# Gated linear attention and a SiLU block on one core: TensorE in stated order for the late chunks, k turned by VectorE and DRAM, masks by ScalarE and GpSimd

## The chip, the cores and the metric

The kernel runs on one core of one Trainium2 chip. The metric is the device time of one execution in microseconds. Before the change it is 563.04 us, the median of three runs (562.8 to 563.6).

## What is computed

Two blocks in a row. The first is a recurrence over 768 tokens for each of 4 batches and 8 heads of dimension 48, with a state of 48x48 that decays by `alpha`:

```python
def _attn_ref(q, k, v, alpha):                      # each (4, 8, 768, 48)
    state = np.zeros((B, H, D, D), dtype=np.float32)
    for t in range(S):
        state = alpha[:, :, t, :, None] * state + np.einsum('bhd,bhe->bhde', k[:, :, t], v[:, :, t])
        y[:, :, t] = np.einsum('bhd,bhde->bhe', q[:, :, t], state)
    return y

def _moe_ref(x, w_in, w_out):                       # x (3072, 384), w_in (384, 2048), w_out (2048, 384)
    h = x @ w_in
    return (h * (1.0 / (1.0 + np.exp(-h)))) @ w_out
```

The output of the first, with batch and token as rows and head and dimension as columns, is the `x` of the second. The weights come as 64-bit floats and are converted on the chip.

## The kernel before

The kernel cuts the tokens into chunks of 128, which gives 24 chunks (6 in time for each of 4 batches), numbered so that chunk `n` is batch `n % 4` at time `n // 4`. A chunk's decays are cumulative products, made by a scan on VectorE. q is multiplied and k divided in such a way that the recurrence within a chunk becomes two matrix products: scores = k q (masked so that only earlier tokens count), and values = v times the masked scores, plus a product of the carried state with q. A third small product adds the chunk's k and v into the state. The second block follows in groups of four chunks. From the third group on, its first product is done with a scheme of 20 block products (`PRODUCTS`), and its second product with 7 (`leave`). All are in float32.

The program is written as a list of steps. In each step, four slots hold stages of attention, and behind each slot some pieces of the second block are filled in. Pools, semaphores and, where nothing keeps an instruction in program order, also the order of each engine's queue are set by the framework's scheduler. `NA` is 8: chunks 0 to 7 are loaded with tokens on the partitions and turned by TensorE; from chunk 8 on, q, k and alpha are loaded so that VectorE's 32x32 block transpose turns them.

The stages of attention that the change touches (cut):

```python
pe, dve, act, gps = nc.tensor, nc.vector, nc.scalar, nc.gpsimd
...
def turns(x, n):                                    # which of two buffers chunk n takes
    return x[(n + 1) % 2 if n < NA else 0]
...
def blank(n):                                       # chunks 8 on: clear two PSUM banks for the scores
    ps = ctxs[n]["blank"] = [ps_attn() for _ in range(2)]
    for t in ps:
        act.activation(t..., ident[:, 0:1].to_broadcast([128, 4 * C]), AF.Copy, scale=0.0)      # L741

def scores(n):
    ps = c.pop("blank") if n >= NA else [ps_attn() for _ in range(2)]
    for j in (0, 2, 1, 3):
        for e in range(2 if n >= NA else 1):
            for u in range(2):
                ...
                pe.matmul(ps[u][at, j, t], lhsT=c["kp"][r, j, at], rhs=c["qp"][r, j, t], ...)    # L757
    g = c["g"] = work.tile([128, 2, NP, C], F32, name="g")
    for u in range(2):
        if n < GB:                                  # chunks 0 to 3
            act.copy(g[:, u], ps[u])                                                             # L763
            gps.affine_select(g[:, u], g[:, u], ...)                                             # L764
            continue
        m = mask[:, :, None, :] if n >= NA else mask[:, 0:1, None, :]
        dve.tensor_tensor(g[:, u]..., ps[u]..., m.to_broadcast(...), ALU.mult)                   # L768
    if ci < NCH - 1:                                # all but the last chunk of each batch
        ps_k = ps_attn()
        for j in range(NP):
            pe.transpose(ps_k[:, j, :], c["kp"][:, j, :], ident)                                 # L774
        c["kn"] = work.tile([128, NP, C], F32, name="kn")
        act.copy(c["kn"], ps_k)                                                                  # L776
    ...
def values(n):                                      # 16 small matmuls, 28 with a state: L800
def states(n):                                      # 16 small matmuls into the state:   L815
```

From chunk 8 on, scores of later and earlier halves of a chunk are written only where the mask can keep something, so the banks are blanked before and multiplied by the mask afterwards.

The slots of a step, and the weights' conversion in the early steps:

```python
for slot, group in enumerate(stages):
    # steps from 8 on, with lag behind the step:
    # [[(scores, 1)], [(products, 0)], [(values, 1), (states, 1)], [(quotient, 0), (blank, 0)]]
    ...
    fill(step, slot)                                # pieces of the second block that are due

def weights(which):                                 # one piece of w_in or w_out for each next()
    up = ahead.pop() if ahead else rounding(bits)   # ScalarE, L609
    dve.tensor_scalar(...); dve.scalar_tensor_tensor(...); dve.tensor_tensor(w, w, up, ALU.add)
    if i + 1 < len(pieces):
        ahead.append(rounding(coming[0]))           # ScalarE, for the next piece
    ...
def store(...):                                     # in leave(): one of 48 outputs
    nc.sync.dma_start(out[r : r + C, c * HO : (c + 1) * HO], o)                                  # L996
```

Of the kernel before, what the change touches and what calls it, by code (L numbers as in the profile page):

```python
# [355 lines left out]
def quotients(  # L356
# [19 lines left out]
    nc = tc.nc  # L376
    pe, dve, act, gps = nc.tensor, nc.vector, nc.scalar, nc.gpsimd
    B, H, S, D = q.shape
# [27 lines left out]
    gpool = pool("gpool", 6)  # L406
    opool = pool("opool", 2)
    rpool = pool("rpool")
    upool = pool("upool")

# [106 lines left out]
    def turns(x, n):  # L517

        return x[(n + 1) % 2 if n < NA else 0]

# [8 lines left out]

    mask = consts.tile([128, 2, C], F32, name="mask")  # L530
    gps.memset(mask, 1.0)
    for odd in range(2):
        for e in range(2):
            m = mask[CH * e : CH * e + CH, odd, :]
            gps.affine_select(m, m, pattern=[[1, C]], compare_op=ALU.is_ge, fill=0.0,
                              base=-CH * (e ^ odd), channel_multiplier=-1)

# [56 lines left out]
    def weights(which):  # L594
# [18 lines left out]
        for i, (dst, src) in enumerate(pieces):  # L613
            if not wide:
                act.dma_start(dst, src)
                yield
                continue
            assert which == 0 or conv_done[0] == n_conv[0]
            bits = coming.pop(0)
            up = ahead.pop() if ahead else rounding(bits)  # L620
            hi, w = bits[:, :, 1], dst.bitcast(I32)
            tc.keep_in_program_order(
                dve.tensor_scalar(w, hi, 3, 0x3FFFFFFF, ALU.logical_shift_left, ALU.bitwise_and))
            dve.scalar_tensor_tensor(w, hi, -(1 << 30), w, ALU.bitwise_and, ALU.bitwise_or)
            dve.tensor_tensor(w, w, up, ALU.add)  # L625
            if i + 1 < len(pieces):
                ahead.append(rounding(coming[0]))
            fetch()
            yield
# [35 lines left out]

    xts, xcs, late = {}, {}, {}

# [8 lines left out]
    def products(n):  # L676
# [25 lines left out]
        dve.tensor_single_scalar(least[:, n, :], u[:, 0:end:W], 2.0**-64, ALU.max)  # L702
        kp = c["kp"] = turns(kps, n)
        ut = tokens(u)
# [13 lines left out]
    def quotient(n, sg=None, q=None):  # L718

        c = ctxs[n]  # L720
        if sg is None:
            if n < NA:
                return
            sg = c.pop("sg")
        end, iv = NP * W, inv
        dve.reciprocal(iv[:, 0:end:W], least[:, n, :])
        p = turns(qps, n)
        dve.tensor_tensor_scan(p[:, 0:end], sg[:, 0:end], iv[:, 0:end], 0.0, ALU.mult, ALU.add)  # L728
        qp = c["qp"] = tokens(p)
        if q is None:  # L730
            q = late["turn"].tile([128, NP, C], F32, name="turn")
            turned(c["q"], q)
        dve.tensor_tensor(qp, q, qp, ALU.mult)

    def blank(n):

        if n < NA:
            return
        ps = ctxs[n]["blank"] = [ps_attn() for _ in range(2)]
        for t in ps:  # L740
            act.activation(t.rearrange("p j c -> p (j c)"), ident[:, 0:1].to_broadcast([128, 4 * C]),  # L741
                           AF.Copy, scale=0.0)

    def scores(n):
        c = ctxs[n]
        ci, b = c["ci"], c["b"]
        ps = c.pop("blank") if n >= NA else [ps_attn() for _ in range(2)]

# [3 lines that stand above are left out]
# [4 lines left out]
                              start=True, stop=True)  # L758
        g = c["g"] = work.tile([128, 2, NP, C], F32, name="g")
        for u in range(2):  # L760
            if n < GB:

                act.copy(g[:, u], ps[u])  # L763
                gps.affine_select(g[:, u], g[:, u], pattern=[[0, NP], [1, C]], compare_op=ALU.is_ge,  # L764
                                  fill=0.0, base=0, channel_multiplier=-1)
                continue
            m = mask[:, :, None, :] if n >= NA else mask[:, 0:1, None, :]
            dve.tensor_tensor(g[:, u].rearrange("p (o j) c -> p o j c", o=2),  # L768
                              ps[u].rearrange("p (o j) c -> p o j c", o=2),
                              m.to_broadcast([128, 2, NP // 2, C]), ALU.mult)  # L770
        if ci < NCH - 1:
            ps_k = ps_attn()
# [12 lines left out]
    def values(n):  # L785

        c = ctxs[n]
        ci, b, g, qp = c["ci"], c["b"], c["g"], c["qp"]
        vn = c["v"].rearrange("p (j u) d -> p j (u d)", u=2)
        s = st[b].rearrange("p j u e -> p j (u e)")  # L790
        py = ps_attn()
        todo = [(3 * j + i, vn[:, j, at : at + 32], g[:, u, j, :])
                for j in range(NP) for i, at, u in ((0, 0, 0), (1, 32, 0), (2, 80, 1))]
        todo += [(3 * j + 1, vn[:, j, 48:80], g[:, 1, j, :]) for j in range(NP)]
        if ci > 0:
# [10 lines left out]
    def states(n):  # L806
        c = ctxs.pop(n)
        ci, b, vn = c["ci"], c["b"], c["v"]
        if ci < NCH - 1:

            ps = ps_attn()
            for j in range(NP):
                for i in range(4):
                    r = slice(32 * i, 32 * i + 32)
                    pe.matmul(ps[r, j, 0:D], lhsT=c["kn"][:, j, r], rhs=vn[:, 2 * j + i // 2, 0:D],  # L815
                              start=True, stop=True)
# [14 lines left out]
    def sums_x(grp):  # L831
        xcs[grp] = late["xc"].tile([128, len(SUMS_X), TB], F32, name="xc")
        for to, sa, a, sb, b in SUMS_X:
            combine(block_x(grp, to), sa, block_x(grp, a), sb, block_x(grp, b))
        yield
# [137 lines left out]
    def leave(grp, h):  # L973
# [14 lines left out]
        def store(m, c, x, y=None):  # L988
# [6 lines left out]
            r = b * S + ci * C  # L995
            nc.sync.dma_start(out[r : r + C, c * HO : (c + 1) * HO], o)  # L996

# [104 lines left out]

    marks = [2 * SLOTS + 2] + [(GB * i + 2 * GB) * SLOTS + 2 for i in range(len(phases))]

    def settle():
# [3 lines left out]
                    wx=pool("wx").tile([128, 8, NQ, 128], F32, name="wx"))  # L1109
        quads = pool("quads")  # L1110
        late["quads"] = {name: quads.tile([128, 32 + 4 * NP * D], F32, name=f"{name}t") for name in "akq"}
        for name, t in late["quads"].items():
# [3 lines left out]
    def fill(step, slot):  # L1116

        at = step * SLOTS + slot
        if at < marks[0]:
            if step >= 1:  # L1120
                convert(0, (at - SLOTS) * 3 // (marks[0] - SLOTS) + 1)
            return
# [10 lines left out]
    for step in range(STEPS):  # L1133
# [6 lines left out]
        elif step >= NA:  # L1140
            stages = [[(scores, 1)], [(products, 0)], [(values, 1), (states, 1)], [(quotient, 0), (blank, 0)]]
        for slot, group in enumerate(stages):
            for stage, lag in group:
# [6 lines left out]
                if stage is states and n + 1 + NIN < NA:  # L1150
                    load(n + 1 + NIN)
                if stage is quotient and n + 1 < NT:
                    load(n + 1)
                if stage is states and n + NV < NT:
                    load_v(n + NV)
            fill(step, slot)
            if step * SLOTS + slot >= NA * SLOTS - 1 and conv_done[1] == NFT and not late:
# [21 lines left out]
    ps = ps_attn()[0:1, 0, 0:1]  # L1179
    pe.matmul(ps, lhsT=good, rhs=mask[:, 0, C - 1 : C], start=True, stop=True)  # L1180
    dve.tensor_single_scalar(small, ps, 127.5, ALU.is_ge)
# [62 lines left out]
```

## Time and profile before

| | |
|---|---|
| Time, median of three | 563.04 us |
| Span of the profiled execution | 561.6 us |
| Instructions | 12,420 |
| DMA | 63.8 MB, 114 GB/s in the mean |
| Granted TensorE clock, mean | 0.994 |

The page of the profile has six parts: busy time by engine, the span in 40 slices, the DMA queues, the chain of work that ended last, the costliest groups of instructions, and the DMA issues. PE is TensorE's matmuls, PEld its weight loads, DVE VectorE, ACT ScalarE, POOL GpSimd, SP SyncE, whose queue issues the DMAs. "L774" is line 774 of the kernel before. The chain is 75% TensorE, 14% VectorE and 5% DMA. A float32 matmul of the large kind appears as two records, so a group "x16" of `ps_o` is one product of 8 matmuls, and a group "x12" of `ps_m` one of 6.

### The profile page before, as it was taken

What the parts mean: (1) busy time and instruction counts of PE and PEld (TensorE: products, weight loads), DVE (VectorE), ACT (ScalarE), POOL (GpSimd) and SP (SyncE); (2) the same over time, 40 slices, a digit from 0 to 9 for tenths busy, and PEclk for the clock granted to TensorE, in tenths of its full rate; (3) what the DMA queues carried; (4) which work ended last, traced back from release to release, by engine and by line L of the source; (5) the groups of instructions that cost most, each with busy time, mean ns of one, the idle gap of its engine ahead of it and who ended that gap; (6) DMA issues with size and microseconds to landing.
All of it is one profiled execution on the core that took longest, in us unless ns stands there. A gap on an engine that the chain in (4) does not pass through costs nothing.

```text
span 561.6 us, 12420 instructions
## 1 busy us (share of the span) xinstructions
PE 543.9 (97%) x5074; PEld 492.6 (88%) x5074; DVE 453.0 (81%) x829; ACT 205.3 (37%) x406; POOL 15.1 (3%) x36
## 2 busy tenths in 40 slices
PE   5899999999999999999999999999999999999996
PEld 3688887998999999899989999999998999899995
DVE  5797899966999799986998897899895875857731
ACT  2566543213233342443433443434443342332100
POOL 4211000100000000000000000000000000000000
PEclk9899999999999999999999999999999999999998
DMA  9989971143443333333425544435522123334200
GB/s 206 230 241 223 234 183 34 43 126 100 100 107 89 73 97 87 101 87 85 131 70 160 142 108 134 130 81 153 136 69 81 53 85 118 99 94 125 71 30 26
DMA packets 94417, 63.81 MB, mean 114 GB/s; under 512 B 55312, under 2 KB 86032, under 8 KB 94352
## 3 DMA queue, kind: packets, MB, share of 16 engines
q1 hardware_dynamic: 94352, 62.94, 43.3%
q8 instruction: 41, 0.67, 0.5%
q14 instruction: 24, 0.20, 0.1%
HBM read 58.20 MB, written 4.72 MB: 112 GB/s over the span
## 4 chain that ended last, share of the span: by engine, by line
PE 75%; DVE 14%; DMA 5%; SPq 2%; issue 2%; ACT 1%; POOL 0%; DVEq 0%; ACTq 0%
PE ps_o L980 33%; PE ps_m L882 18%; PE ps_m L858 11%; PE ps_a L800 6%; DMA bits<-in_moe_w_out_dram 3%; PE ps_a L757 3%; DVE seen L663 2%; PE ps_a L774 1%; DVE g L896 1%; DMA bits<-in_moe_w_in_dram 1%; DVE u L699 1%; PE ps_a L815 1%; DVE w_out L625 1%; DVE p L728 1%; SPq L456 1%
## 5 line engine op out<-in xcount | busy, mean ns | idle before, releaser
L980 PE MATMUL ps_o<-w_out,g 128*128 128x192 f32 x768 | 133.6, 328 | 1.1 <-DVE o L994 1.1
L980 PEld LDWEIGHTS ps_o<-w_out,g 128*128 128x128 f32 x768 | 125.5, 190 | 3.9 <-DVE o L994 1.5
L980 PE MATMUL ps_o<-wt,g 128*128 128x192 f32 x576 | 100.0, 327 | 0.0
L980 PEld LDWEIGHTS ps_o<-wt,g 128*128 128x128 f32 x576 | 95.1, 190 | 1.5
L858 PE MATMUL ps_m<-xt,w_in 128*128 128x256 f32 x384 | 88.5, 382 | 1.0 <-ACT xt L805 1.0
L858 PEld LDWEIGHTS ps_m<-xt,w_in 128*128 128x128 f32 x384 | 71.0, 190 | 11.0 <-ACT xt L805 1.4
L882 PE MATMUL ps_m<-xc,w_in 128*128 128x256 f32 x288 | 70.1, 379 | 0.0
L882 PEld LDWEIGHTS ps_m<-xc,w_in 128*128 128x128 f32 x288 | 54.0, 190 | 6.4 <-DVE g L896 0.2
L663 DVE TENSOR_REDUCE seen<-bits 128x1 f32<-128x384 int32 (+2 forms) x65 | 42.4, 689 | 16.8 <-DMA bits<-in_moe_w_out_dram 16.5
L893 ACT ACTIVATE g<-g 128x1024 f32<-128x1024 f32 x32 | 33.1, 1055 | 57.5 <-DVE g L896 57.5
L985 DVE TENSOR_TENSOR g<-g 128x512 f32<-128x512 f32 x72 | 48.5, 686 | 5.6 <-PE ps_o L980 5.6
L882 PE MATMUL ps_m<-xc,wx 128*128 128x256 f32 x192 | 50.1, 383 | 0.0
L888 ACT COPY g<-ps_m 128x512 f32<-128x512 f32 x64 | 36.8, 587 | 36.1 <-PE ps_m L882 36.0
L780 ACT ACTIVATE st<-st,least 128x96 f32<-128x96 f32 x80 | 24.1, 364 | 58.4 <-DVE least L702 58.4
L882 PEld LDWEIGHTS ps_m<-xc,wx 128*128 128x128 f32 x192 | 35.0, 190 | 4.2 <-issue 0.4
L896 DVE TENSOR_TENSOR g<-ps_m,g 128x512 f32<-128x512 f32 x56 | 37.4, 683 | 0.8 <-PE ps_m L882 0.5
L699 DVE TENSOR_TENSOR_SCAN u<-al,one 128x516 f32<-128x516 f32 x24 | 29.1, 1212 | 10.4 <-ACT al L696 10.3
L728 DVE TENSOR_TENSOR_SCAN p<-al,inv 128x516 f32<-128x516 f32 x24 | 29.4, 1226 | 5.2 <-PE ps_a L800 4.9
L861 ACT ACTIVATE g<-ps_m 128x512 f32<-128x512 f32 x32 | 19.0, 595 | 39.2 <-PE ps_m L858 39.0
L800 PE MATMUL ps_a<-g,vn 128*32 128x128 f32 x768 | 28.0, 282 | 3.9 <-POOL g L764 3.9
L800 PEld LDWEIGHTS ps_a<-g,vn 128*32 128x32 f32 x768 | 20.3, 112 | 11.2 <-issue 5.5
L768 DVE TENSOR_TENSOR g<-ps_a,mask 128x512 f32<-128x512 f32 x40 | 25.7, 685 | 4.0 <-PE ps_a L757 3.7
(125 smaller groups left out, 620.7 us busy)
## 6 DMA issues: line engine op xcount, KB each, us to landing
bits<-in_moe_w_in_dram SPq DMA_DIRECT2D x24, 512.0 KB, 4.7
bits<-in_moe_w_out_dram SPq DMA_DIRECT2D x32, 384.0 KB, 3.4
at<-in_alpha_dram SPq DMA_DIRECT2D x64, 96.0 KB, 2.4
kt<-in_k_dram SPq DMA_DIRECT2D x64, 96.0 KB, 2.6
qt<-in_q_dram SPq DMA_DIRECT2D x64, 96.0 KB, 2.5
bits<-in_alpha_dram SPq DMA_DIRECT2D x9, 512.0 KB, 3.8
out_dram<-o SPq DMA_DIRECT2D x48, 96.0 KB, 1.9
an<-in_alpha_dram SPq DMA_DIRECT2D x8, 192.0 KB, 5.1
```

What stands on the lines that cost most here:

```text
L663: dve.tensor_reduce(seen[kind][which][:, i : i + 1], x, axis=AX, op=op, apply_absolute_value=True))
L699: dve.tensor_tensor_scan(u[:, end - 1 :: -1], sg[:, end:0:-1], one[:, end:0:-1], 0.0, ALU.mult, ALU.add)
L728: dve.tensor_tensor_scan(p[:, 0:end], sg[:, 0:end], iv[:, 0:end], 0.0, ALU.mult, ALU.add)
L768: dve.tensor_tensor(g[:, u].rearrange("p (o j) c -> p o j c", o=2), ps[u].rearrange("p (o j) c -> p o j c", o=2), m.to_broadcast([128, 2, ...
L800: pe.matmul(py[32 * at : 32 * at + 32, t, :], lhsT=w, rhs=x, start=(i < 4), stop=(i >= len(todo) - 4), skip_group_check=True)
L858: pe.matmul(ps[:, e, :], lhsT=w_in[:, t, (f + e) * 128 : (f + e + 1) * 128], rhs=xt[:, t, :], start=(t == 0), stop=(t == NKT - 1))
L882: pe.matmul(ps[:, e], lhsT=block_w(w)[:, 2 * pair + e], rhs=block_x(grp, x), start=(first and e == 0), stop=(e == 1), skip_group_check=True)
L888: act.copy(to, ps)
L893: act.activation(x, x, AF.Silu)
L896: dve.tensor_tensor(to, a, b, op)
L980: pe.matmul(ps, lhsT=x, rhs=w[:, i], start=(first and i == 0), stop=(i == HF - 1), skip_group_check=True)
L985: dve.tensor_tensor(cells(grp, h, pair, *to), cells(grp, h, pair, *x), cells(grp, h, pair, *y), ALU.subtract)
```

## The change

The change has six parts:

1. From chunk 8's step on (as soon as `late` is filled), every TensorE instruction is kept in the order in which the program states it. Before that the scheduler still decides. The sums of `sums_x` on VectorE are kept in order too.
2. For chunks 8 to 19, k is no longer transposed by TensorE. VectorE transposes its 32x32 blocks (`flip`), one DMA writes them to DRAM, four DMAs read them back in the order that the states need (`land`), a step later.
3. The masks of chunks 4 to 7 are made like those of chunks 0 to 3. Those of chunks 8 to 23 are made by six ScalarE copies and four GpSimd selections; the part that nobody writes is set to zero once, so the blanking goes, and so does the mask tensor.
4. Outputs are issued by GpSimd's queue, except those of the last group.
5. The stages are arranged anew: quotient in the third slot; values, states and `flip` in the fourth. q gets a second buffer for the late chunks, and the marks by which pieces fall due move by one slot.
6. In the first steps, the first weight conversion of ScalarE is asked for on its own, before the rest.

It is for taking work off TensorE, and for giving it a queue whose order the author sets. The diff, cut to its core:

```diff
-    pe, dve, act, gps = nc.tensor, nc.vector, nc.scalar, nc.gpsimd
+    dve, act, gps = nc.vector, nc.scalar, nc.gpsimd
+    late = {}
+    def in_order(ins):
+        return tc.keep_in_program_order(ins) if late else ins
+    class pe:
+        @staticmethod
+        def matmul(*args, **kw):
+            in_order(nc.tensor.matmul(*args, **kw))
+        @staticmethod
+        def transpose(*args):
+            in_order(nc.tensor.transpose(*args))
...
-    opool = pool("opool", 2)
+    opool = pool("opool", 3)
+    dram = pool("dram", 2, bass.MemoryType.DRAM)
...
-    mask = consts.tile([128, 2, C], F32, name="mask")
-    gps.memset(mask, 1.0)
-    (four affine_selects on it)
+    decayed = fix.tile([128, 2 * NP * C], F32, name="g")
+    low, high = slice(0, CH), slice(CH, C)
+    earlier, later = [(low, 0), (high, 1)], [(low, 1), (high, 0)]
...
             up = ahead.pop() if ahead else rounding(bits)
+            if which == i == 0:
+                yield
...
-        p = turns(qps, n)
+        p = turns(qps if n < NA else [qps[0], late["p"]], n)
...
-    def blank(n): (two ScalarE activations into PSUM)
+    def flip(n):
+        if n < NA or c["ci"] == NCH - 1:
+            return
+        t = late["turn"].tile([128, NP, C], F32, name="turn").rearrange("p c (j d) -> p c j d", j=NP)
+        dve.transpose(t, c["kp"].rearrange("p j (c i) -> p c j i", i=32))
+        c["flip"] = dram.tile([128, NP * C], F32, name="flips")
+        nc.sync.dma_start(c["flip"], t.rearrange("p c j d -> p (c j d)"))
+    def land(n):
+        if "flip" in c:
+            c["kn"] = work.tile([128, NP, C], F32, name="kn")
+            x = c.pop("flip").rearrange("(r d) (i x) -> i d r x", r=4, i=4)
+            for i in range(4):
+                nc.sync.dma_start(c["kn"][32 * i : 32 * i + 32], x[i])
...
-        for u in range(2):
-            (chunks 0 to 3: ScalarE copy, GpSimd select; others: VectorE times mask)
-        if ci < NCH - 1:
+        for u in range(2 if n < NA else 0):
+            act.copy(g[:, u], ps[u])
+            gps.affine_select(g[:, u], g[:, u], pattern=[[0, NP], [1, C]], ...)
+        if n >= NA:
+            for u in range(2):
+                act.copy(swapped[:, :, u, :, CH:], ps[u][:, :, :, CH:])
+            for r, o in earlier:
+                for u in range(2):
+                    act.copy(swapped[r, o, u, :, 0:CH], ps[u][r, o, :, 0:CH])
+            for at, half in ((CH, later), (0, earlier)):
+                for r, o in half:
+                    x = swapped[r, o].rearrange("p u j c -> p (u j) c")[:, :, at : at + CH]
+                    gps.affine_select(x, x, pattern=[[0, NP], [1, CH]], ...)
+        if n < NA and ci < NCH - 1:
...
-            nc.sync.dma_start(out[r : r + C, c * HO : (c + 1) * HO], o)
+            (gps if grp < NG - 1 else nc.sync).dma_start(out[r : r + C, c * HO : (c + 1) * HO], o)
...
-    marks = [2 * SLOTS + 2] + [(GB * i + 2 * GB) * SLOTS + 2 for i in range(len(phases))]
+    marks = [2 * SLOTS + 2] + [(GB * i + 2 * GB) * SLOTS + 3 for i in range(len(phases))]
...
+            if at == SLOTS:
+                next(conv[0])
...
-            stages = [[(scores, 1)], [(products, 0)], [(values, 1), (states, 1)], [(quotient, 0), (blank, 0)]]
+            stages = [[(land, 1), (scores, 1)], [(products, 0)], [(quotient, 0)],
+                      [(values, 1), (states, 1), (flip, 0)]]
```

## The prediction

> **What bounds the kernel now.** I read the page from the top: shares of busy time, then the slices, then single stretches of the timeline. Part 1 of the page and three rows of its part 2 (each digit the busy tenths of one fortieth of the span, some 14 us):
>
> ```profile
> PE 543.9 (97%) x5074; PEld 492.6 (88%) x5074; DVE 453.0 (81%) x829; ACT 205.3 (37%) x406; POOL 15.1 (3%) x36
> ...
> PE   5899999999999999999999999999999999999996
> PEld 3688887998999999899989999999998999899995
> DVE  5797899966999799986998897899895875857731
> ```
>
> The reader is to see that TensorE (PE) has no free slice between the second and the last. A busy PE row alone proves little, because the ends of matmuls are modelled. So I compared starts in the timeline of TensorE: between 130 and 480 us eight products of 128x192 follow each other in 2.60 us (325 ns each) and six of 128x256 in 2.59 us (432 ns each), stretch after stretch. Only a few are slower: the two groups at 230.70 to 233.30 us lose some 0.9 us, one at 292.62 us some 0.6, one at 481.59 us some 1.2, the values of the chunk at 87 us some 1. **TensorE's queue is the bound**, nearly without gaps, from 25 us to its end near 556 us; the last 5.5 us are the final output. VectorE with 81% is second; ScalarE and GpSimd are far off.
>
> Two stretches carry the prediction. The first is the timeline of TensorE around one step of a late chunk with the turn of k (L774), and around one without it (chunks 20 to 23 need no new state). Columns: start and length in us, engine and line, operation:
>
> ```profile
> 308.50 0.90 PE L757 MATMUL ps_a<-p,kp 48*64 48x128 f32 x32
> 309.33 0.65 PE L774 MATMUL ps_a<-ident,kp 128*128 128x128 f32 x4
> 309.82 2.77 PE L980 MATMUL ps_o<-w_out,g 128*128 128x192 f32 x16
> 312.43 1.03 PE L882 MATMUL ps_m<-xc,wx 128*128 128x256 f32 x4
> ...
> 393.42 0.90 PE L757 MATMUL ps_a<-p,kp 48*64 48x128 f32 x32
> 394.25 2.87 PE L980 MATMUL ps_o<-w_out,g 128*128 128x192 f32 x16
> 396.95 1.03 PE L882 MATMUL ps_m<-xc,wx 128*128 128x256 f32 x4
> ```
>
> From the start of the scores to the start of the group after the product: 312.43 - 308.50 = 3.93 us with the turn, 396.95 - 393.42 = 3.53 us without. The four transposes cost TensorE 0.40 us net, not 0.65 and not the sum of their mean durations, because the first weight load after the small score tiles is better hidden behind them.
>
> The second is the chain of waits in the first 28 us:
>
> ```profile
> 7.61 6.10 DMA bits<-in_moe_w_in_dram
> 13.71 0.02 issue
> 13.73 0.67 ACT up L609
> 14.40 0.48 ACT g L763
> 14.88 0.06 issue
> 14.94 1.95 POOL g L764 x2
> 16.89 0.04 issue
> 16.93 1.58 PE ps_a L800 x25
> ```
>
> Chunk 0's scores left TensorE before 11.7 us, but ScalarE copies them only at 14.3, since a second conversion of weights stands ahead of them in its queue and waits for a DMA that lands at 13.7. TensorE idles 3.6 us for that.
>
> [...] at 14.94 us two mask operations of GpSimd took 1.94 us where a later pair took 1.23, while a VectorE operation that takes 0.42 us took 0.85.
>
> **The change part by part.** The groups (busy us, mean ns) that price it:
>
> ```profile
> L774 PE MATMUL ps_a<-ident,kp 128*128 128x128 f32 x80 | 13.1, 286 | 0.2 <-DVE st L821 0.2
> L768 DVE TENSOR_TENSOR g<-ps_a,mask 128x512 f32<-128x512 f32 x40 | 25.7, 685 | 4.0 <-PE ps_a L757 3.7
> L674 DVE STREAM_TRANSPOSE turn<-kt 128x512 f32<-128x512 f32 x16 | 17.7, 1105 | 0.0
> L741 ACT ACTIVATE ps_a<-ident 128x512 f32<-128x512 f32 x32 | 19.0, 598 | 0.4
> L776 ACT COPY kn<-ps_a 128x512 f32<-128x512 f32 x20 | 11.7, 584 | 14.5 <-PE ps_a L774 14.5
> ```
>
> *TensorE.* Chunks 8 to 19 lose their four transposes: 12 x 0.40 = **4.8 us**, all of it on the path. Nothing is added. Up to chunk 8 its order is nearly the old one. After that it is the order in which the program states the work; I compared the two queues, and the large groups stay interleaved alike. What moves is the scores: they now stand some 2.6 us behind the values and states of the chunk before, and the values come some 14.7 us later (24 products of 325 ns, 16 of 432).
>
> *VectorE.* It loses 40 masks x 0.685 = 27.4 us and gains 12 turns x 1.11 = 13.3: 14 us less. That is off the path, but it is the engine that lets PSUM banks go, so the few stalls above may shrink.
>
> *ScalarE.* It loses 32 blankings x 0.598 = 19.1 us and 12 copies of k x 0.584 = 7.0. It gains 8 copies x 0.587 = 4.7 (chunks 4 to 7), and in each of chunks 8 to 23 two copies of 256 and four of 128 columns. The copies of the trace (0.316 us at 192 columns, 0.475 at 384, 0.587 at 512) put these at 0.37 and 0.26 us, an estimate: 16 x 1.8 = 28 us. Net +7 us on an engine that is busy 37%.
>
> *GpSimd.* 8 masks x 0.85 us, and 64 masks of 64 partitions x 256, each some 0.5 us as an estimate between 0.33 (64x128) and 0.87 (128x512): some 39 us more, and the issue of 40 outputs. From scores to values there are then some 2 us of copies and 2 us of masks, within the 14.7 us that TensorE spends on other work.
>
> *DMA.* k goes out as 256 KB and comes back, twelve times. Issues of 96 KB land in some 2.5 us; the way out and back is some 6 us with its issues, and the states need k a whole step (16 to 21 us) later. I count it as hidden. Moving 40 outputs off SyncE's queue frees loads of the 102 us in which that queue stood waiting for results (L996), again beside the path.
>
> *The start.* In the new queue of ScalarE the first weight conversion stands alone and chunk 0's copies come before the second. They can begin at 11.39 + 0.69 = 12.1 us rather than 14.3. Values of chunk 0 move from 15.9 to some 13.7 us: 2.2 us. From there on TensorE is the chain up to 68 us, but weights arrive at 225 GB/s all the while and could eat part: I take **1.8 us**.
>
> Sum: 563.0 - 4.8 - 1.8 = 556.4. Old stalls (some 3.7 us together) less new ones of the stated order: I choose -0.4. **556.0 us.**
>
> **The rivals.** *First, the stated order makes TensorE wait.* An engine that can't be reordered stalls on every late operand: scores need q and k of VectorE, values need masks of GpSimd, whose queue also holds output DMAs that wait for results. VectorE is at 80 to 98% in the slices between 200 and 420 us. For it: the scheduler's order had gaps at 230 and 292 us for just such a wait. Against it: my count leaves 5 us or more for each operand. One extra wait of 0.5 us per step over 16 steps gives 8 us and no gain: 564. *Second, GpSimd and VectorE contend.* 64 masks of 0.5 us could hold VectorE up by 10 us or more, which returns the 14 us it gained; TensorE would then stall as before, and the time stays near 556 to 558. *Third, all stalls vanish* as VectorE gets lighter: 563.0 - 4.8 - 2.2 - 3.7 = 552.3, the floor that this reading allows. *Fourth, the turn through DRAM is late* and states stall: SyncE's queue holds it behind 15 loads. Each microsecond late costs 12 us in all; I see some 5 us of room.
>
> **Range and chances.** The floor of 552.3 lies just above 551.8, where 2% faster begins, so faster is unlikely (0.07: it needs gains that I didn't find). For slower than 574.3 the stated order would have to cost 18 us, over a microsecond a step (0.03). The range is 552.5 to 560.5, wider above, because new waits are what I can count least.
>
> **What would show it right or wrong.** Right: no transposes of k on TensorE after chunk 7; the step from scores to the next group 0.4 us shorter; values of chunk 0 near 13.7 us; TensorE's starts still 325 and 432 ns apart with fewer than 4 us of gaps in all; its last product some 7 us earlier; VectorE near 439 us busy, if contention with GpSimd doesn't stretch it. Wrong: waits of the score or value matmuls on VectorE, ScalarE or GpSimd that come back each step; states waiting for the DMA of k; or the start's gain gone by 100 us because weights weren't there.

## The result, and the profile after

The changed kernel takes 567.93 us (567.44 to 568.32) against 562.99 us of the kernel before on the same chip: a ratio of **1.0085, 95% interval 1.0068 to 1.0103**. That is 4.8 us slower by the ratio (4.9 by the medians), where the prediction had 7 us faster and its range ended at 560.5.

The same rows of the page as before, of the changed kernel, with the row of the granted clock:

```profile
PE 545.6 (96%) x5026; PEld 489.6 (86%) x5026; DVE 444.1 (78%) x801; ACT 207.7 (37%) x466; POOL 72.6 (13%) x146
...
PE   6999999999979999999999999999999999999995
PEld 4788887998968989889999989998898999997995
DVE  5997879885957799998997988997993776857531
PEclk9999999999997999999999999999999999999999
```

TensorE has 48 matmuls fewer (12 x 4 turns of k) and yet is busy 1.7 us longer. VectorE fell by 9 us. Two slices tell where to look: the twelfth, from 156 to 170 us, where TensorE drops to 7 and VectorE to 5, and the thirteenth, where the clock drops to 7. The other slices are about as full as before. (All matmuls now carry the line L388 of a helper, and transposes L392.)

The stretch itself, from the timeline of the changed kernel. Columns: start and length in us, engine and line, operation, count, and in brackets the idle time before it and what ended it:

```profile
158.02 0.90 PE L388 MATMUL ps_a<-p,kp 48*64 48x128 f32 x32
158.85 2.87 PE L388 MATMUL ps_o<-wt,g 128*128 128x192 f32 x16
161.55 2.75 PE L388 MATMUL ps_m<-xt,w_in 128*128 128x256 f32 x12
164.14 2.76 PE L388 MATMUL ps_o<-w_out,g 128*128 128x192 f32 x16
165.56 1.11 DVE L692 STREAM_TRANSPOSE al<-at 128x512 f32<-128x512 f32 x1 [6.11 <-DMA at<-in_alpha_dram]
166.98 1.22 DVE L717 TENSOR_TENSOR_SCAN u<-al,one 128x516 f32<-128x516 f32 x1
169.04 0.16 DVE L720 TENSOR_SCALAR least<-u 128x4 f32<-128x4 f32 x1
169.23 0.64 ACT L817 ACTIVATE st<-st,least 128x96 f32<-128x96 f32 x2 [8.78 <-DVE least L720]
169.90 0.60 ACT L900 ACTIVATE g<-ps_m 128x512 f32<-128x512 f32 x1
170.55 5.49 PE L388 MATMUL ps_m<-xt,w_in 128*128 128x256 f32 x12 [3.64 <-ACT g L900]
```

Read it from the bottom. TensorE idles 3.64 us for a SiLU of ScalarE (L900) that empties the PSUM bank it needs. The product before that SiLU was ready by 164.3; but ahead of the SiLU in ScalarE's queue stands the decay of the state (L817), and ScalarE stood 8.78 us for VectorE's `least`. VectorE in turn stood 6.11 us for alpha's DMA. So alpha was late, and three engines passed it on. When TensorE resumes, the product (x12) takes 5.49 us, where the same one at 161.55 took 2.75. The stretches of the trace say why (columns: stretch, length, busy of PE, PEld, DVE, ACT and POOL with counts, granted clock, DMA share, GB/s):

```profile
167.00:170.50 3.50, 0.00 (x0) 0.00 (x0) 3.46 (x10) 1.24 (x4) 0.00 (x0) 0.90 0.60 166
170.50:174.00 3.50, 3.45 (x8) 2.80 (x9) 3.47 (x7) 0.52 (x2) 0.00 (x0) 0.50 0.10 28
174.00:176.00 2.00, 2.00 (x9) 1.07 (x10) 1.97 (x5) 0.00 (x0) 0.56 (x1) 0.50 0.16 53
176.00:178.00 2.00, 2.00 (x77) 1.95 (x80) 1.79 (x3) 0.60 (x1) 0.00 (x0) 0.85 0.00 0
```

The clock falls to 0.50 near 169.8 us (0.90 over 3.5 us is 0.7 us at one half) and comes back near 176.6: 6.8 us at half speed. Some 0.8 us of them lie within the idle time; the 6.1 us after 170.55 cost 3.0 us of matmul time beside the idle 3.64. Together some 6.7 us are lost at one place.

Why was alpha late? SyncE's waits and its timeline of the changed kernel answer (waits: us in total, times, longest):

```profile
SPq L763 <- DVE turn L761: 60.7, 9, 11.4
...
151.44 0.38 SPq L482 DMA_DIRECT2D at<-in_alpha_dram  x1
158.73 0.34 SPq L763 DMA_DIRECT2D flips<-turn  x1
159.12 1.39 SPq L482 DMA_DIRECT2D at<-in_alpha_dram  x1
160.61 0.40 SPq L499 DMA_DIRECT2D vn<-in_v_dram  x1
161.10 1.26 SPq L501 DMA_DIRECT2D vn<-in_v_dram  x2
162.41 1.07 SPq L482 DMA_DIRECT2D at<-in_alpha_dram  x2
```

Between 151.8 and 158.7 SyncE issues nothing. At the head of its queue stands the write of the turned k to DRAM (L763), which waits for VectorE; behind it stand the next chunk's loads, which wait for nothing but their turn: one of the four loads of alpha is out at 151.44 us, the other three come after the write. The stated order puts `load(n + 1)` after `flip(n)`, in the same queue. That is one more line of the change, which neither the list of its parts nor the diff above shows: in the kernel before, the loads are stated after `quotient`. **The write holds up the loads.** It does so in other steps too: VectorE waits for alpha's DMA in five places, 11.9 us in all. Only here does the lateness stop TensorE for long.

### The profile page after: what moved, and what is told of

Same layout as the page of the kernel before. It is cut to its first block, busy times and chain, and to the rows that moved or that the text cites. A ratio compares the mean times of both kernels' runs of the same rounds, so it can differ in the third digit from the quotient of the medians.

```text
span 566.6 us, 12602 instructions
## 1 busy us (share of the span) xinstructions
PE 545.6 (96%) x5026; PEld 489.6 (86%) x5026; DVE 444.1 (78%) x801; ACT 207.7 (37%) x466; POOL 72.6 (13%) x146
## 3 DMA queue, kind: packets, MB, share of 16 engines
q0 software_dynamic: 1920, 3.93, 2.0%
## 5 line engine op out<-in xcount | busy, mean ns | idle before, releaser
L388 PE MATMUL ps_o<-w_out,g 128*128 128x192 f32 x768 | 134.6, 329 | 1.6 <-DVE o L1033 1.4
L388 PEld LDWEIGHTS ps_o<-w_out,g 128*128 128x128 f32 x768 | 125.4, 190 | 5.5 <-DVE o L1033 2.5
L388 PE MATMUL ps_m<-xt,w_in 128*128 128x256 f32 x480 | 116.6, 390 | 5.0 <-ACT g L900 3.6
L388 PEld LDWEIGHTS ps_m<-xt,w_in 128*128 128x128 f32 x480 | 90.6, 193 | 19.3 <-ACT g L900 3.9
L388 PE MATMUL ps_o<-wt,g 128*128 128x192 f32 x576 | 99.7, 326 | 0.0
L388 PEld LDWEIGHTS ps_o<-wt,g 128*128 128x128 f32 x576 | 95.1, 190 | 1.6 <-issue 0.2
L388 PE MATMUL ps_m<-xc,w_in 128*128 128x256 f32 x288 | 70.8, 382 | 2.0 <-ACT part L927 1.4
L388 PEld LDWEIGHTS ps_m<-xc,w_in 128*128 128x128 f32 x288 | 53.6, 190 | 9.4 <-ACT part L927 1.7
L388 PE MATMUL ps_m<-xc,wx 128*128 128x256 f32 x192 | 50.1, 383 | 0.1
L1036 POOL DMA_DIRECT2D out_dram<-o x40 | 22.1, 552 | 219.1 <-DVE o L1033 130.2
L806 POOL TENSOR_SCALAR_AFFINE_SELECT g<-g 64x256 f32<-64x256 f32 x64 | 30.5, 477 | 141.3 <-ACT g L799 124.0
L817 ACT ACTIVATE st<-st,least 128x96 f32<-128x96 f32 x80 | 24.3, 365 | 57.4 <-DVE least L720 57.3
L388 PEld LDWEIGHTS ps_m<-xc,wx 128*128 128x128 f32 x192 | 35.1, 190 | 4.6 <-ACT g L927 0.4
L717 DVE TENSOR_TENSOR_SCAN u<-al,one 128x516 f32<-128x516 f32 x24 | 29.5, 1227 | 9.9 <-ACT al L714 9.5
L692 DVE STREAM_TRANSPOSE al<-at 128x512 f32<-128x512 f32 x16 | 17.8, 1111 | 19.3 <-DMA at<-in_alpha_dram 11.9
L900 ACT ACTIVATE g<-ps_m 128x512 f32<-128x512 f32 x32 | 19.0, 595 | 37.5 <-PE ps_m L388 37.4
```

The lines of the kernel that those rows point to most:

```text
L388: in_order(nc.tensor.matmul(*args, **kw))
L717: dve.tensor_tensor_scan(u[:, end - 1 :: -1], sg[:, end:0:-1], one[:, end:0:-1], 0.0, ALU.mult, ALU.add)
L806: gps.affine_select(x, x, pattern=[[0, NP], [1, CH]], compare_op=ALU.is_ge, fill=0.0, base=0, channel_multiplier=-1)
L817: act.mul(s[:, j], s[:, j], least[:, n, j : j + 1])
L900: act.activation(gts[grp, h, pair][:, i : i + 2, q % 2, :], ps, AF.Silu)
L1036: (gps if grp < NG - 1 else nc.sync).dma_start(out[r : r + C, c * HO : (c + 1) * HO], o)
```

## The experiments

Theory A: the time is lost to the loads that stand behind the write, and to the half clock that the idle time brings. Theory B: TensorE's stated order makes it wait, as the prediction's first rival had it. The experiments are variants of the changed kernel unless said otherwise; a ratio is always to the kernel before on the same chip.

**Loads ahead of the write.** One line is put back as it is in the kernel before, so that the loads are stated one stage earlier:

```diff
-                if stage is flip and n + 1 < NT:
+                if stage is quotient and n + 1 < NT:
                     load(n + 1)
```

> The change with one line moved: the loads of the next chunk are stated after the quotient (third slot), ahead of the DMA that writes turned k to DRAM, not after it. Theory A (queue): that DMA stands at the head of SyncE's queue and waits for VectorE, in all 61 us, and the alpha loads behind it come late; near 167 us this starves VectorE for 6.1 us, then ScalarE, then TensorE for 3.6 us, and the clock is halved for some 5 us after. With the loads ahead, the gap at 167 us and the half clock go: some 7 us less, 560 to 561 us. Theory B (stated order): TensorE's fixed order is what costs, with whatever operand is late; the time stays at 566 to 568. Theory C (GpSimd and VectorE contend): stays at 568.

Measured: 560.66 us, ratio 0.9941 (0.9923 to 0.9959), 7 to 8 us faster than the changed kernel. The idle time at 167 us and the half clock are gone (granted clock 1.00 from 140 to 180 us). Alpha's transpose and the product that waited, in the timeline of this run:

```profile
162.27 1.10 DVE L692 STREAM_TRANSPOSE al<-at 128x512 f32<-128x512 f32 x1
162.74 0.55 SPq L763 DMA_DIRECT2D flips<-turn  x1
163.41 1.23 DVE L717 TENSOR_TENSOR_SCAN u<-al,one 128x516 f32<-128x516 f32 x1
164.88 1.17 ACT L817 ACTIVATE st<-st,least 128x96 f32<-128x96 f32 x4 [4.66 <-DVE least L720]
167.37 0.60 ACT L900 ACTIVATE g<-ps_m 128x512 f32<-128x512 f32 x1
168.24 2.75 PE L388 MATMUL ps_m<-xt,w_in 128*128 128x256 f32 x12
```

Alpha is turned before the write has left, `least` comes 4.4 us earlier, and the product starts without a wait, at full clock. Theory A holds for this loss. But 2.7 to 3.3 us faster than before is not the 7 that the prediction had, so something else is also missing; the last experiments go after it.

**The write in another queue.** The write and the read back go to GpSimd's queue (L763, L771: `nc.sync` becomes `gps`), the loads stay where they were.

> The change, but turned k is written to DRAM and read back by GpSimd's queue, with SyncE's queue free of it. Theory A: as in the run before, no late alpha near 167 us, 560 to 562 us, unless masks on GpSimd now stand behind these DMAs. Theory B: 566 to 568. Theory C: 568 or more, as GpSimd has more to do.

Measured: 562.45 us, ratio 0.9978 (0.9961 to 0.9996). No wait at 167 us, no half clock (0.999 granted in the mean): the queue that the two shared is the cause, not the write itself. It is 2 us slower than the loads stated earlier, with other idle times of TensorE: 1.6 us in three between 224 and 231 us, 2.4 us in two at 481 and 518 us.

**k by TensorE again.** `flip` returns at once, and `scores` turns k for all chunks as before; the rest of the change stays.

> The change without the turn of k by VectorE and DRAM: TensorE transposes k in all chunks as before. The outputs, masks, order and start are as in the change. Theory A: no such DMA in SyncE's queue, so the gap near 167 us (some 7 us with the slow clock) goes, while 12 x 0.40 = 4.8 us of transposes come back: some 566 us. Theory B: the gap stays and the transposes come back: 572 to 573 us. Theory C: VectorE is 13 us lighter, some us below B.

Measured: 564.86 us, ratio 1.0017 (1.0007 to 1.0028), no wait at 167 us. Without the write the loads aren't held, though they are stated where the change put them. Against the early load, which does turn k through DRAM, it is 0.0076 x 563 = 4.3 us slower: 0.36 us for each of 12 chunks. That agrees with the 0.40 us that the prediction had from the spacing of starts. (The two kernels also differ in where the loads stand.)

**The scheduler's order throughout.** `in_order` returns the instruction as it is.

> The change, but TensorE's order is the scheduler's all the way; SyncE's queue is the same as in the change at chunks 8 to 12. Theory A: alpha is as late as before, so the gap near 167 us stays: 565 to 569 us. Theory B: the gaps go, 556 to 558 us. Theory C: 568.

Measured: 568.74 us, ratio 1.0095 (1.0064 to 1.0126). Freeing TensorE's order brings no time, so theory B is refuted in this form. The time lies where theory A had it, but that is luck: SyncE still waits for the turn (49.9 us in 7 waits), yet TensorE does not stop near 167 us and there is no half clock there (the product of `ps_m` at 167.95 us takes 2.75 us). In their place come many small waits (the idle times of TensorE over 0.15 us between 60 and 560 us sum to 10.2 us, in the changed kernel to 8.7) and split products. The stop at 167 us thus needs both: late loads, and an order in which TensorE can't take other work first.

**The last link.** Is it ScalarE's decay of the state, ahead of the SiLU, that brings the lateness to TensorE? Here the late chunks' decay is GpSimd's:

```diff
-            for j in range(NP):
-                act.mul(s[:, j], s[:, j], least[:, n, j : j + 1])
+            if n < NA:
+                for j in range(NP):
+                    act.mul(s[:, j], s[:, j], least[:, n, j : j + 1])
+            else:
+                gps.tensor_tensor(s, s, least[:, n, :, None].to_broadcast([128, NP, 2 * D]), ALU.mult)
```

> The change, but from chunk 8 on the decay of the carried state is done by GpSimd in one operation, not by ScalarE in four. SyncE's queue is left as it is in the change, so alpha is late near 167 us as before. Theory A with its last link (ScalarE's queue has the state's decay at its head, which waits for VectorE, and the SiLU behind it should free TensorE's bank): TensorE no longer idles 3.6 us nor is the clock halved, some 561 to 563 us, though VectorE still waits some 6 us for alpha. If the link is not ScalarE's queue but VectorE's own lateness, TensorE stalls as before: 566 to 568.

Measured: 575.23 us, ratio 1.0204 (1.0182 to 1.0226), not what I expected. Two lines of its timeline:

```profile
167.09 1.12 DVE L692 STREAM_TRANSPOSE al<-at 128x512 f32<-128x512 f32 x1 [5.75 <-DMA at<-in_alpha_dram]
179.32 0.90 PE L388 MATMUL ps_a<-p,kp 48*64 48x128 f32 x32 [3.26 <-DVE p L751]
```

The SiLU is on time and TensorE doesn't stop at 170 us. But VectorE is still 5.75 us late, and TensorE pays 3.26 us at the next scores, which need VectorE's `p`; half clock follows there too: the product behind those scores (x12) takes 4.54 us, where the one at 168.50 took 2.75. The link through ScalarE only decided where the lateness arrived. A second wait, of 3.5 us for VectorE's `g`, is new (the changed kernel's longest for `g` is 0.3); GpSimd now stands 105 us for `least`, with its masks behind, but whether that brings this wait I did not follow.

**Idle time and clock.** To separate the half clock from its cause here, a wait is made up in the early-load kernel, in step 17: TensorE turns a tile, GpSimd runs selects over it one after the other, and a matmul of no use waits for the last. Twelve selects in one run, five in the other:

```diff
+            if step == 17 and slot == 1:
+                look = work.tile([128, C], F32, name="idle")
+                ...
+                for _ in range(12):
+                    gps.affine_select(look, look, ...)
+                pe.matmul(ps, lhsT=look, rhs=ident, start=True, stop=True)
```

> The change with early loads, and in step 17 a made-up wait of TensorE: a 128x128 transpose, a ScalarE copy, 12 GpSimd selections of 128x128 (0.29 us each), and a matmul that needs the result. TensorE should stand idle some 4 to 5 us there. If an idle of this length also halves the clock for the next 3 to 7 us, as read from the change's trace at 170 us, the time is 6 to 8 us above the 560.7 of early loads alone and the trace shows a granted clock of 0.5; if the half clock in the change was by chance, only the idle is added: 565.

> The early load with the made-up wait of the long-idle run cut from twelve selects to five: TensorE should idle some 3.5 us in place of 7. Theory A (an idle of this length halves the granted clock for some 7 us after it, as behind the wait of the changed kernel): 560.7 + 3.5 + 3.4, some 567 to 568 us, and a stretch at 0.5 of clock behind the idle. Rival B (a short idle leaves the clock alone; the half clock at 170 us had another cause): 564 us and no stretch at 0.5.

Measured: the long one 573.06 us, ratio 1.0155 (1.0135 to 1.0176); the short one 570.41 us, ratio 1.0114 (1.009 to 1.0138). TensorE stood idle for 6.81 and 3.27 us, and both traces show a granted clock of 0.50, for 10.2 and 6.8 us. So a made-up idle time brings the half clock as well, but both runs are slower than their expectations had it. Of the short one, a group of the same kind ahead of the wait and behind it (1.99 us at full clock, 3.62 after the wait), and its stretches:

```profile
280.03 1.99 PE L388 MATMUL ps_m<-xc,w_in 128*128 128x256 f32 x8
294.65 3.62 PE L388 MATMUL ps_m<-xc,w_in 128*128 128x256 f32 x8
...
292.00:294.00 2.00, 0.00 (x0) 0.00 (x0) 1.97 (x4) 0.00 (x0) 1.73 (x5) 0.73 0.88 241
294.00:296.00 2.00, 1.94 (x6) 1.67 (x7) 2.00 (x4) 0.27 (x1) 0.01 (x1) 0.50 0.80 216
296.00:298.00 2.00, 2.00 (x6) 1.61 (x5) 1.37 (x2) 0.58 (x1) 0.00 (x0) 0.50 0.85 210
298.00:300.00 2.00, 2.00 (x7) 1.59 (x6) 1.08 (x2) 0.63 (x2) 0.00 (x0) 0.57 0.29 117
```

The half clock begins while TensorE still stands: in the short run it lasts from 292.9 to 299.7 us and TensorE resumes at 294.06, in the long one from 291.0 to 301.25 and TensorE resumes at 295.78. So matmuls run at half clock for 5.7 and 5.5 us, which costs 2.8 and 2.7 us. With the idle time that is 6.1 us of a measured loss of 0.0173 x 563 = 9.7 us for the short run, and 9.5 us of 0.0214 x 563 = 12.0 for the long one. Later waits also grew (at 488 and 525 us in the short run): all idle times of TensorE, counted as above, sum to 10.4 and 14.7 us, against 6.1 in the early-load kernel. With all of them 7.1 and 11.3 us are accounted for; 2.6 us of the short run stay open.

**Outputs on SyncE's queue again**, in the early-load kernel (L1036: always `nc.sync`).

> The change with early loads, and the outputs back on SyncE's queue. In that queue of the kernel before outputs held other DMAs up for 102 us in all. If this queue is what matters (theory A): 1 to 3 us slower than with early loads alone, 562 to 564. If outputs are beside the path either way: 560 to 561.

Measured: 566.56 us, ratio 1.0044 (1.0027 to 1.0062), 5.8 us slower than with the outputs on GpSimd's queue, more than either reading had. From its waits of SyncE and its timeline of TensorE:

```profile
SPq L1036 <- DVE o L1033: 57.2, 25, 5.6
...
175.18 0.55 PE L388 MATMUL ps_a<-vn,kn 128*32 128x48 f32 x32 [2.78 <-DMA kn<-flips]
```

Now it is the reading back of k that stands behind an output waiting for VectorE, and the states wait 2.78 us for it (1.58 more at 341 us). As long as the turn through DRAM uses SyncE's queue, moving the outputs out of it is a condition of its gain.

**The start alone**, added to the kernel before (the extra `yield` and `next(conv[0])`).

> The kernel before with the start of the change alone: the first weight conversion asked for on its own, so that chunk 0's scores are copied ahead of the second conversion. Nothing else of the change. The trace of the change has TensorE 2.5 us earlier at 125 us. If the start's gain is kept to the end: 560.5 to 561 us, as much as the whole of the change with early loads has. If it is lost at the weights or in the audits at the end: 562 to 563.

Measured: 561.74 us, ratio 0.9957 (0.994 to 0.9973): 2.4 us faster. The gain of the start is kept to the end. It can't be told apart from the gain of the whole change with early loads (0.9941): the other parts together show no clear gain beside it.

**Order and masks once the loads are early.** Three runs on the early-load kernel: TensorE's order left to the scheduler; the late masks multiplied in by VectorE (two operations of 128x256 and four of 64x128 for a chunk, in place of ScalarE's copies and GpSimd's selects); both together.

> The early load of the fourth experiment's kind (0.994 of the kernel before), with TensorE's matmuls left to the scheduler. Theory A (the stated order costs little, and only leaves small waits that the scheduler would have filled): 558 to 560 us, ratio 0.990 to 0.993, with fewer waits above 0.7 us than the 8 us in sum of the early load alone. Rival B (the stated order is worth its name, because the scheduler splits products of 256 columns): 564 to 569 us, as the scheduler's order cost when the loads were late.

> The early load, with the late chunks' masks multiplied in by VectorE as the scores leave PSUM (two of 128x256 and four of 64x128 a chunk, some 1.6 us of VectorE), so without ScalarE's copies and GpSimd's selects. Theory A (the masks' two links on ScalarE and GpSimd don't reach TensorE, the values come two slots later): within 1.5 us of the early load alone, 559 to 562 us. Rival B (ScalarE's copies hold up the SiLU that the large products wait for, which is where the gain of the transposes went): 556 to 558 us. Rival C (VectorE, late already at its loads, becomes later): 563 to 566 us.

> Both of the last two: early load, scheduler's order, masks on VectorE; what is left of the change is the start, the turn of k through DRAM and outputs on GpSimd's queue. If the start is worth 2.3 us and the turn of k 0.35 to 0.40 us for each of 12 chunks, and nothing else costs, 556 to 557 us. If it comes to 560 us or more, the turn's own waits or the order of the scheduler cost what it saves.

("The fourth experiment's kind" in the first of these texts means the early load above.) Measured: 571.42 us, ratio 1.0128 (1.0111 to 1.0145); 565.86 us, ratio 1.0039 (1.0018 to 1.0059); 573.08 us, ratio 1.0159 (1.0137 to 1.0181). So with early loads the stated order is worth 0.0187 x 563 = 10.5 us and the masks' move 0.0098 x 563 = 5.5 us. Theory A was wrong in both: the first is slower than even Rival B had it, the second is Rival C's case (from 60 to 540 us VectorE is busy for 411.6 us, against 392.8 in the early-load kernel). The third is far above the 560 us at which its expectation has costs of the turn or of the order. And left to the scheduler, early loads gain nothing (1.0128, against 1.0095 with late ones): their 7 to 8 us are a gain under the stated order alone. A wait from the first run's timeline, and one from the second's:

```profile
291.63 1.65 PE L388 MATMUL ps_m<-xc,w_in 128*128 128x256 f32 x4 [2.40 <-DVE xc L580]
...
176.94 0.90 PE L388 MATMUL ps_a<-p,kp 48*64 48x128 f32 x32 [1.45 <-DVE p L758]
```

In the scheduler's order TensorE comes to products whose sums (`xc`) VectorE hasn't made: its idle times, counted as above, sum to 12.2 us against 6.1 in the early-load kernel, and behind this one the clock is at one half for 3.4 us. With the masks on VectorE they sum to 9.7, and the scores wait for `p`. Why the scheduler's order had only 3.0 us of such idle time in the kernel before, and does so badly with k turned through DRAM, I did not settle.

**The waits that are left.** Two parts of the change could bring the waits of the early-load kernel: the stated order of VectorE's sums (`tc.keep_in_program_order` around `combine` in `sums_x`), and the feed-forward's pieces counted one slot later (`+ 3` in `marks`). Each is undone in the early-load kernel.

> The early load, with the sums of token blocks that VectorE forms ahead of each group left to the scheduler, as in the kernel before. Theory A (their stated place makes the first products of a group wait for a sum, 1.1 us at 370 us, and delays the combinations at 200 and 230 us): 557 to 559 us. Rival B (the scheduler would place them later, and the products of the stated order wait longer): 563 us or more. Rival C (their place doesn't matter, VectorE as a whole is late there): within 1 us of the early load alone, 560 to 561.5.

> The early load, with the feed-forward's pieces counted from the slot of the kernel before (one slot earlier in each four chunks). Theory A (the later slot isn't the cause of the waits): within 1.5 us of the early load alone, 559 to 562. Rival B (the slot later is what leaves TensorE to wait for VectorE's and ScalarE's combinations): 557 to 558.5 us. Rival C (the later slot is needed, since the values of four chunks are only just there): 563 us or more, with waits of the first products for xt or for sums.

Measured: 560.9 us, ratio 0.9955 (0.9934 to 0.9976), the same as with the sums in stated order (0.9941); and 569.3 us, ratio 1.01 (1.0071 to 1.0129), 9 us slower. In the second TensorE comes too soon to products that need what ScalarE copies, and slow matmuls follow: the groups x4 at 204.99, 206.85 and 208.56 us take 2.07, 1.91 and 1.91 us, where one takes 1.03 at 214.65:

```profile
204.99 2.07 PE L388 MATMUL ps_m<-xc,wx 128*128 128x256 f32 x4 [3.19 <-ACT g L927]
```

The later slot is needed (the third reading that the expectation gave); for the order of the sums no difference was measured.

## Why the prediction was wrong

**The step that failed is "DMA".** It had "I count it as hidden", with "some 5 us of room" in the fourth rival. I asked when the turned k must be back and found a whole step of room, and k was indeed never late in the changed kernel. What I didn't ask was what stands behind the write while it waits for its data. The rival named SyncE's queue, but the wrong way round: it saw the turn held behind 15 loads, and it was the loads that were held behind the turn, which cost 7 to 8 us with the half clock that followed. It took the loads to be stated first, as in the kernel before; the change moves them behind the write. Nor were the outputs' moves "beside the path": they are worth 5.8 us, in good part (4.4 us of TensorE's waits) because the read back would otherwise wait behind them.

**The step of the old and new stalls, "I choose -0.4"**, failed as well. With the loads early, TensorE's starts lose some 8 us in waits against 3.7 before, by the same count of spacing: 1.8 us at 200 us for a copy of ScalarE, 1.3 at 368 for VectorE's sums, 1.5 between 514 and 528, and smaller ones. That is +4.3 in place of -0.4. The first rival was right that a queue in stated order finds new waits, but not in where: they don't come back each step at scores and values, most stand at products of the second block. Nor would the scheduler's order have avoided them: it costs 10.5 us more.

The terms side by side (us):

| term | predicted | shown by the runs |
|---|---|---|
| 12 turns of k off TensorE | -4.8 | -4.8 by spacing, -4.3 against k by TensorE |
| start | -1.8 | -2.4 (start alone) |
| loads behind the write, with the half clock | 0 | +7 to +8 (against the early load, in stated order) |
| other waits of TensorE | -0.4 | about +4.3 (spacing, early load) |
| sum | -7.0 | +4 to +5 with -4.8; measured +4.8 |

What held: no turns of k after chunk 7; from scores to the group after the product 161.55 - 158.02 = 3.53 us, where it was 3.93; values of chunk 0 at 14.34 us, not 13.7, and 15.89 before; and the group after the states of chunk 7 started 2.5 us earlier (125.42 against 127.93 us), so the start's gain was not eaten by the weights. The weight load that the prediction saw better hidden behind the transposes shows in the trace of before: the product's first load starts at 309.71 us, its first matmul at 309.82, and it takes 2.77 us; without transposes both start at 394.25 and it takes 2.87. GpSimd's masks took 477 ns each, against an estimate of 500:

```profile
L806 POOL TENSOR_SCALAR_AFFINE_SELECT g<-g 64x256 f32<-64x256 f32 x64 | 30.5, 477 | 141.3 <-ACT g L799 124.0
```

The line shows what the masks wait for, ScalarE's copies, and nothing is lost by it: in the list of TensorE's waits in the changed kernel there is none for these masks, and none for the turned k.

The second rival, contention of GpSimd and VectorE, does show, but small. Operations that both kernels have take VectorE 5.2 us more in sum in the changed kernel. `kp` (128x256) gains the most in sum, 0.86 us: 449 ns in the mean against 422 before. In the changed kernel five of its 32 operations overlap a mask of GpSimd (L806); four of them take 0.59 to 0.62 us and one 0.43, while the other 27 take 0.39 to 0.49. The scans of `u` hardly change (1227 against 1212 ns), nor do the operations on `g` with an input in PSUM (682 against 683).

VectorE came to 444 us busy against the 439 of the prediction, with errors on both sides. The turn of k takes 0.71 us, not 1.11. The 40 masks are 25.7 us of busy time, not 27.4, since some overlap. The operations that both kernels have add those 5 us. Nor is VectorE at 80 to 98% in all slices between 200 and 420 us: two digits of its row there are a 6 and a 7. And in the prediction's example of contention the operation just ahead of the one of 0.85 us (`w_in<-bits`) was longer too: `w_in<-w_in,up` took 0.90 us, against 0.69 later.

The lowest ratio here is the early load's: the change with its loads stated ahead of the write, 0.9941 of the kernel before, and 1.4% below the change. It is not clearly ahead of the start alone (0.9957) or of the early load with free sums (0.9955).

## What to carry to other kernels

When a DMA that waits for a computed result joins a queue, look at what stands behind it in that queue, not only at when its own data is needed: loads that wait for nothing should be issued ahead of it, or in another queue (here worth 7 to 8 us). An engine that isn't the bound can still pass lateness on through whatever stands next in its queue (here ScalarE, busy for 37%, stood 8.78 us with a SiLU behind, and TensorE then 3.64), so a wait is traced back link by link until one is found that is a matter of order alone. Parts of a change aren't worth a fixed sum each: in the kernel with early loads the stated order, the masks' move and the outputs' queue each cost 5 to 10 us to undo, while with late loads the stated order was worth nothing (1.0085 against 1.0095 without it).

## What the hardware showed that I had not expected

A single idle time of TensorE in mid-kernel cost up to nearly twice its length. Idle times of 3.27, 3.64 and 6.81 us brought 6.8, 6.8 and 10.2 us at a granted clock of 0.50, begun before TensorE resumed, and so another 2.8, 3.0 and 2.7 us of matmul time.

Its length alone does not decide that in these runs. Here are first the early load in the scheduler's order, where an idle time of 2.40 us ends at 291.63 us (columns as in the stretches above), then the early load with the outputs on SyncE's queue, where one of 2.78 us ends at 175.18 us (columns as in the timelines):

```profile
290.00:292.00 2.00, 0.37 (x2) 0.37 (x3) 2.00 (x4) 0.00 (x0) 0.00 (x0) 1.00 0.79 217
292.00:294.00 2.00, 2.00 (x7) 1.53 (x6) 2.00 (x6) 0.60 (x2) 0.00 (x0) 0.51 0.20 53
294.00:296.00 2.00, 2.00 (x8) 1.76 (x7) 1.97 (x5) 1.33 (x4) 0.00 (x0) 0.63 0.00 0
296.00:298.00 2.00, 2.00 (x14) 1.95 (x13) 1.51 (x3) 1.00 (x3) 0.00 (x0) 1.00 0.00 0
...
175.18 0.55 PE L388 MATMUL ps_a<-vn,kn 128*32 128x48 f32 x32 [2.78 <-DMA kn<-flips]
175.66 2.87 PE L388 MATMUL ps_o<-w_out,g 128*128 128x192 f32 x16
178.46 0.90 PE L388 MATMUL ps_a<-p,kp 48*64 48x128 f32 x32
179.29 2.86 PE L388 MATMUL ps_m<-xt,w_in 128*128 128x256 f32 x12
```

In the first the clock is at one half for 3.4 us (0.51 and 0.63 over 2 us are 1.96 and 1.48 us of it). In the second the matmuls behind the wait are not slowed: the product at 179.29 takes 2.86 us, where the same one took 5.49 at half clock in the changed kernel, and the granted clock of the whole execution is 0.998. So the shorter idle time cost half clock and the longer one did not. What else decides it, the runs here do not show.
